# Old sums copied into PSUM by ScalarE, and four plain chunks instead of eight, in a fused attention and mixer block

## Chip, cores and metric

The kernel runs on one NeuronCore of one Trainium2 chip. The metric is device time in microseconds (us) for one execution. TensorE (PE) multiplies matrices into PSUM; VectorE (DVE), ScalarE (ACT) and GpSimd (POOL) do the rest; SyncE (SP) issues most DMAs. PEld is the weight load of TensorE.

## What is computed

```python
x = A_x                                   # 1 x 2048 x 576, float32
xn = _layernorm(x)
return x + _A_ref(xn, A_wqkv, A_wo) + _B_ref(xn, B_w1, B_w2, B_w3, B_w4)
```

`_A_ref` is attention with 32 heads of 18 channels, in which every token looks at 8 tokens: itself and those 2, 4, ... 14 places before it. `_B_ref` is a mixer: `h = gelu(layernorm(xn) @ w1)`, four channel groups shifted by 1, -1, 2, -2 tokens, `x1 = xn + hs @ w2`, and then `x1 + gelu(layernorm(x1) @ w3) @ w4` with a hidden width of 4608.

## The kernel before, in words

**Precision.** Every float32 operand is kept as a high part (rounded to `float32r`) and a low part (the remainder), and a product is three products: high by high, high by low, low by high. A contraction over 576 channels is therefore 14 matmuls (`PAIRS`), one over 128 hidden channels 3. Making the two parts is a cast on ScalarE and a subtraction on VectorE; the functions named `split_...` and `low_part` (L815) do that.

**Stages.** First QKV: for each tile of 128 tokens, `q_half` (L319) makes one half of the 1728 columns at a time, 864 of them, as two accumulations of 432 columns in two PSUM banks (`mm_tok`, L211); ScalarE copies them out (L323) and they are stored to `qkvd` in DRAM. Tiles 4 to 15 go this way, the first four through `q_cg`. Then the first mixer (L466 to L500), then `w2` (the loop at L621), whose result is the running sum `Y`, 16 tiles of 128 tokens. Then the hidden layer of the second mixer, which is by far the longest stage, and at last the product with `wo` (L1335 on).

**The running sum.** For the tiles in `YD` (1, 2, 3, 5, 7, 9, 10, 11, 13, 15) the sum lives in DRAM (`yd`), and the space of these tiles in `Y` serves as scratch (`temp`; the raw W4 is loaded to the places of tiles 1 and 3). The other six tiles (0, 4, 6, 8, 12, 14) are summed in `Y` in SBUF. `down` (L830) makes the contribution of 256 hidden channels to one tile: 12 matmuls of 288 columns into a two-bank PSUM tile. For a YD tile ScalarE copies it out (L846), and GpSimd issues a DMA that adds it to `yd` (L847). For another tile VectorE adds PSUM to `Y` (L851).

**The hidden layer** has 36 blocks of 128 hidden channels; two make a chunk, 18 chunks. The first `NPL` (8) are *plain*: a unit is one chunk by 512 tokens. In a unit, two `up`s (L819) of 14 matmuls of 512 columns each give the hidden values, ScalarE applies GELU twice from PSUM (L805, L806), VectorE makes the low part (L817), and then four downs follow for the unit before (`prev`). PSUM tiles of the downs come from a pool of three (`psb`).

The other chunks (`NWP`, 10) use a fast scheme with seven products instead of eight: two chunks' worth of output, 256 hidden channels by 1024 tokens, is one *step* `q` of the loop at L1140, 2 x `NWP` steps in all, the first `NWP` for the first half of the tokens (`sb` 0), the others for the second. `product` (L1069) is 7 matmuls of 512 columns. Their weights are sums and differences made on chip: `load_pair` (L915) loads a pair of blocks into the staging tile `w3st` (one buffer), `split_a` (L944) makes the operands A (`w3a`, two buffers), `combine` (L926) forms the differences in place on VectorE, `split_s` (L950) makes the operands S (`w3s`). In `split_ws` (L934) step 0 is a cast (L936) and step 1 another cast and a GpSimd DMA that accumulates (L939). The token operands (`B11`, `B21`, `T1` ... `T4`, `B22`) are loaded by `get_op` (L885) and split by `split_op` (L895), seven for each half; the sums `T` over normalised tokens are made in DRAM by `sums` (L868).

**The order of a step** is written out by hand as a string (`ORDER`, L1135, and `ORDERS` for steps 0, `NWP` - 1 and `NWP`): P1 to P7 are the seven products and D0 to D7 the eight downs of the step before. What else is done after which item stands in `plan` (`at(...)`, L1174 on). P1, P6, P7 and P4 add up in one PSUM bank (`ca`), and in between `keep` (L1080) copies the bank to SBUF: P1 gives Z1, P6 gives Z2, P7 gives Z3. P2 and P1 together give hidden values: P2 has its own bank, VectorE adds it to Z1 (`z_add`, L1083), and `gelu_z` (L809) takes them from SBUF. The same is done for Z2 and Z3 with P3's bank. The downs have two PSUM tiles (`qpd`). Every engine works through its instructions in the order in which they are written, with waits on semaphores.

**Attention** (L677) runs on VectorE in the background from unit 2 on, eight groups of four heads. It is a generator; each `yield` names the cost of what it has issued in us, and `bg` (L772) lets it go on while its budget lasts: 9.4 us per plain unit (`RATE`), and 1.6 us less what is already `spent` per item of a step. `av` sums the weighted values of a group in `po[:, 0]` and stores it to `od`. The softmax's exp is on ScalarE (L755). In step `NQ` - 6, after P4, whatever is left is done at once, and `od` is loaded, transposed and split for the last product.

Of the kernel before, what the change touches and what calls it, by code (L numbers as in the profile page):

```python
# [19 lines left out]
HD = 18  # L20
# [16 lines left out]
NPL = 8  # L37
# [20 lines left out]
def fused_block(ctx, tc, x, wqkv, wo, w1, w2, w3, w4, out):  # L58
# [487 lines left out]
    def split_w3(f):  # L546
        if f // 2 % 2 == 0:
            W3[f] = wp.tile([128, 15, 128], F32R, name="w3a", bufs=2)[:, 0:10, :]
        elif f % 2 == 0:
            t = wspool.tile([128, 20, 128], F32R, name="w3s")  # L550
            W3[f], W3[f + 1] = t[:, 0:10, :], t[:, 10:20, :]
        split_w(W3[f][:, 0:5, :], W3[f][:, 5:10, :], raws[f])
# [124 lines left out]
    def attention(ap):  # L677
# [8 lines left out]
        o = po[:, 0, :].rearrange("p (x d) -> p x d", d=HD)  # L686
# [12 lines left out]
        def av(g):  # L699
            if g == NG - 1:  # L700
                exp_now()
            L, v = Ls[g], vs[g]
            Lf = L.rearrange("p j h w -> p (j h) w")
# [6 lines left out]
            for w in range(W):  # L710
# [5 lines left out]
                if w:  # L716
# [3 lines left out]
                         po[:, 0, :].rearrange("p (j c) -> p j c", c=GC))  # L720
# [107 lines left out]
    nps = [0]  # L828

    def down(t, parts, pd):  # L830
        col = slice(t % 4 * 128, (t % 4 + 1) * 128)
        if pd is None:
            nps[0] += 1
            ps = qpd.tile([128, 2, 512], F32, name=f"ps{nps[0] % 2}")
        else:
            ps = pd.tile([128, 2, 512], F32, name="ps", tag="b")
# [3 lines left out]
        for n, (h, w, p) in enumerate(seq):  # L840
            for k in range(2):
                pe.matmul(ps[:, k, :HF], h[:, col], w[:, p, k * HF:(k + 1) * HF],  # L842
                          start=n == 0, stop=n == len(seq) - 1)
# [4 lines left out]
        else:  # L848
            spent[0] += 0.75
            yv = Y[:, t, :].rearrange("p (h c) -> p h c", h=2)  # L850
            dve.tensor_tensor(yv, ps[:, :, :HF], yv, op=ALU.add)  # L851
# [11 lines left out]
    def add_x(t):  # L863
        if t not in YD:
            dve.tensor_tensor(Y[:, t, :], Y[:, t, :], xagain[t], op=ALU.add)
# [97 lines left out]
    RATE = [9.4, 0.0]  # L963
# [5 lines left out]

    for u, (c, b) in enumerate(units):  # L970
        if u == 2:
# [9 lines left out]
        for i in range(C):  # L981
            bg(r, False)
# [28 lines left out]
        for j, (t, parts) in enumerate(prev):  # L1011
            bg(r, j % 2 == 1)
            down(t, parts, psb)
# [7 lines left out]
            for f in {(-3, 1): (lambda: split_a(0),), (-3, 3): (lambda: combine(0),),  # L1021
# [14 lines left out]
        if z == -5:  # L1036
            load_pair(0)
        if z == -3:
# [5 lines left out]
        if z == -2:  # L1044
# [5 lines left out]
            load_w4(NPL)  # L1050
        if 5 <= u < 21 and u % 2:
            sums((u - 5) // 8, (u - 5) % 8 // 2)
        if 13 <= u < 13 + NT:
            load_xa(u - 13)
        if 14 <= u < 14 + NT:
            add_x(u - 14)
# [6 lines left out]
    qpd = qpdc.__enter__()  # L1063
    Z1, Z2, Z3, Z4 = temp(13), temp(15), temp(5), temp(7)
# [22 lines left out]
    def downs(g):  # L1087
        s0 = 8 * (g // NWP)
        w1, w0 = W4[2 * (NPL + pair(g))], W4[2 * (NPL + pair(g)) + 1]
        for j in range(8):  # L1090
            if j < 4:
                yield lambda j=j: down(s0 + 4 + j, [(hid[g, "c12"], w0), (hid[g, "c22"], w1)], None)
            else:
                yield lambda j=j: down(s0 + j - 4, [(hid[g, "c11"], w0), (hid[g, "c21"], w1)], None)

    def plain_downs():
        for t, parts in prev:
            yield lambda t=t, parts=parts: down(t, parts, None)
# [31 lines left out]
    def o_turn(t):  # L1130
# [4 lines left out]
    ORDER = "P1 P2 D0 P6 D1 P5 D2 P7 D3 P4 D4 P3 D5 D6 D7"  # L1135
    ORDERS = {0: "P1 P2 D0 P6 P5 P7 D1 D2 P3 P4 D3",
              NWP - 1: "P1 P2 P6 P5 P7 D0 P4 P3 D1 D2 D3 D4 D5 D6 D7",
              NWP: "D0 D1 P1 P2 D2 P6 D3 P5 P7 D4 P4 P3 D5 D6 D7"}
    spent[0] = 0.0
    for q in range(NQ):  # L1140
# [36 lines left out]
        if q == 0:  # L1177
            at("P2", split_op, 0, "B22")
            at("P5", split_op, 0, "T4")
            at("P7", split_a, n, (0, 1))  # L1180
            at("D1", gelu22)
            at("D1", split_a, n, (2,))
            at("D2", low22)
            at("P3", combine, n)
# [4 lines left out]
            at("D3", split_w4, p)  # L1189
            at("D3", load_pair, q + 2)  # L1190
        elif q == NWP - 1:
# [5 lines left out]
            at("D0", split_op, 1, "B11")  # L1197
# [23 lines left out]
        elif z < -1:  # L1221
# [6 lines left out]
            at("P4", split_w4, p, 1)  # L1228
            at("D4", low22)
# [162 lines left out]
```

## Time and profile before

| | us |
|---|---|
| median of 3 runs | 1294.18 (1293.34 to 1298.37) |
| the profiled execution's own time | 1294.18 |
| its span, first to last instruction | 1292.4 |
| TensorE busy | 1267.1 |
| VectorE busy | 944.7 |
| ScalarE busy | 598.7 |
| GpSimd busy | 246.3 |

The mean granted TensorE clock is 0.994 of full speed; in the page's 40 slices it is full except for one in the middle of the last third. The difference between the execution's time and the span is what lies around the first and last instruction. QKV ends at about 195 us of the span, the plain stage runs from about 313 to 719 and the steps from there to about 1215, with the last downs to 1230.

How to read the rows that follow: a row of the timeline is start, duration, engine, line, operation, output and inputs, shape and count, and in brackets the idle time before it and what ended it. Neighbouring instructions of one kind are merged. A row of the groups ends with total busy time, mean ns of one, and the idle time before. A row of the waits is total, times and longest. A row of the windows is the stretch, its length, and the busy time of PE, PEld, DVE, ACT and POOL, then granted clock, DMA share and GB/s. A row of the DMA issues ends with the KB of one and the median us from issue to landing. Matmuls overlap, so their pace is read from start to start and not from their duration.

### The profile page before, as it was taken

The numbers are of one execution on the slowest core, as the hardware profiler recorded it, in microseconds if no ns is written. First come the engines' busy times: TensorE is split into PE (matmuls) and PEld (weight loads), VectorE is DVE, ScalarE is ACT, GpSimd is POOL, SyncE is SP. The second block draws the span as 40 slices with busy tenths as digits, with TensorE's granted clock in tenths as the row PEclk, the third lists the DMA queues.
The fourth block names the chain that finished last, engine by engine and source line by source line (L and its number), as shares of the span: only waits on it lengthen the run. The fifth ranks groups of instructions, "written<-read, shape, count | busy, mean of one in ns | idle before, by whom it ended". The sixth has DMA issues, their size and how long they took to land.

```text
span 1292.4 us, 19686 instructions
## 1 busy us (share of the span) xinstructions
PE 1267.1 (98%) x7538; PEld 1163.1 (90%) x7538; DVE 944.7 (73%) x1261; ACT 598.7 (46%) x952; POOL 246.3 (19%) x358
## 2 busy tenths in 40 slices
PE   8999999999999999999999999999979999999999
PEld 8999998899898998999999799989968999988998
DVE  6456534778469999999999789989978554566542
ACT  3322126526634434343345746546547555555530
POOL 2011100021221212231212212222212222222100
PEclk9999999999999999999999999999989999999999
DMA  7646874246886878989788767686595757799972
GB/s 210 156 113 139 171 173 143 73 131 174 220 245 148 180 165 202 229 154 222 136 200 204 168 136 163 112 191 154 106 261 87 155 102 154 178 218 222 254 250 83
DMA packets 201374, 219.16 MB, mean 170 GB/s; under 512 B 79152, under 2 KB 137744, under 8 KB 201152
## 3 DMA queue, kind: packets, MB, share of 16 engines
q1 hardware_dynamic: 168912, 151.57, 40.9%
q0 software_dynamic: 32368, 66.34, 32.2%
q8 instruction: 59, 0.97, 0.3%
q14 instruction: 35, 0.29, 0.1%
HBM read 119.73 MB, written 107.28 MB: 176 GB/s over the span
## 4 chain that ended last, share of the span: by engine, by line
PE 74%; DMA 8%; issue 7%; DVE 6%; ACT 2%; SPq 2%; POOL 1%; DVEq 0%; POOLq 0%; ACTq 0%
PE ps L842 26%; PE ps L214 16%; PE cc L1075 12%; PE p L823 12%; PE ps L466 4%; PE ps L313 3%; DMA yd<-Y 2%; DMA w3st<-in_B_w_dram 1%; DMA Y<-in_B_w_dram 1%; DMA w3a<-w3st 1%; DVE w L569 1%; DMA od<-po 1%; PE ps L481 1%; DVE w3st L931 1%; DMA w3s<-w3st 1%
## 5 line engine op out<-in xcount | busy, mean ns | idle before, releaser
L842 PEld LDWEIGHTS ps<-w,c 128*128 128x128 f32 x3456 | 474.9, 188 | 28.1 <-DVE Y L851 7.7
L842 PE MATMUL ps<-w,c 128*128 128x288 f32 x3456 | 486.4, 295 | 11.9 <-DVE Y L851 5.6
L847 POOL DMA_DIRECT2D yd<-Y x154 | 137.3, 897 | 453.9 <-ACT Y L846 378.6
L846 ACT COPY Y<-ps 128x576 f32<-128x576 f32 x154 | 98.1, 637 | 141.8 <-PE ps L842 90.4
L817 DVE TENSOR_TENSOR c<-Y,c 128x512 fp32r<-128x512 f32 x144 | 98.5, 685 | 60.0 <-ACT Y L806 49.9
L214 PE MATMUL ps<-WQ,xt 128*128 128x432 f32 x672 | 134.8, 360 | 0.0
L214 PEld LDWEIGHTS ps<-WQ,xt 128*128 128x128 f32 x672 | 125.6, 188 | 5.7
L851 DVE TENSOR_TENSOR Y<-ps,Y 128x576 f32<-128x576 f32 x108 | 81.1, 751 | 48.8 <-PE ps L842 48.5
L1075 PE MATMUL cc<-xt,w3s 128*128 128x512 f32 x420 | 108.8, 400 | 0.0
L737 DVE TENSOR_TENSOR po<-q,k 128x2304 f32<-128x2304 f32 (+1 forms) x40 | 82.9, 2073 | 16.1 <-issue 10.9
L805 ACT ACTIVATE c<-p 128x512 fp32r<-128x512 f32 x64 | 38.3, 599 | 119.3 <-PE p L823 119.3
L1075 PEld LDWEIGHTS cc<-xt,w3s 128*128 128x128 f32 x420 | 77.4, 192 | 14.1 <-DVE Y L1085 0.2
L740 DVE TENSOR_REDUCE L<-po 128x128 f32<-128x2304 f32 (+1 forms) x40 | 82.7, 2068 | 0.4
L1081 ACT COPY Y<-cc 128x512 f32<-128x512 f32 x60 | 35.1, 585 | 100.7 <-PE cc L1075 94.9
L121 POOL TENSOR_TENSOR rs<-rs,mhalf 128x1 f32<-128x1 f32 x48 | 31.6, 659 | 258.1 <-DVE rs L120 147.8
L717 DVE TENSOR_TENSOR po<-po 128x1152 f32<-128x1152 f32 x56 | 75.8, 1353 | 0.9
L713 DVE TENSOR_TENSOR po<-v,L 128x1152 f32<-128x1152 f32 x56 | 75.6, 1352 | 0.7
L323 ACT COPY stg<-ps 128x864 f32<-128x864 f32 x24 | 21.2, 882 | 102.8 <-PE ps L214 55.8
L1075 PE MATMUL cc<-x1n,w3a 128*128 128x512 f32 (+1 forms) x280 | 67.9, 393 | 0.0
L1075 PEld LDWEIGHTS cc<-x1n,w3a 128*128 128x128 f32 (+1 forms) x280 | 51.6, 188 | 10.3
L214 PE MATMUL ps<-W,h 128*128 128x288 f32 x384 | 53.5, 295 | 0.0
L823 PE MATMUL p<-xt,w3s 128*128 128x512 f32 x224 | 52.4, 390 | 0.0
(189 smaller groups left out, 1904.3 us busy)
## 6 DMA issues: line engine op xcount, KB each, us to landing
yd<-Y POOLq DMA_DIRECT2D x156, 288.0 KB, 5.3
Y<-in_B_w_dram SPq DMA_DIRECT2D x27, 576.0 KB, 6.9
w3st<-in_B_w_dram SPq DMA_DIRECT2D x52, 256.0 KB, 6.4
qkvd<-stg SPq DMA_DIRECT2D x24, 432.0 KB, 3.5
yd<-ev POOLq DMA_DIRECT2D x26, 288.0 KB, 6.2
xd<-st SPq DMA_DIRECT2D x16, 320.0 KB, 6.0
xd<-big SPq DMA_DIRECT2D x16, 320.0 KB, 7.9
w3st<-in_B_w_dram SPq DMA_DIRECT2D x76, 64.0 KB, 6.6
```

Of the source, the lines that this page charges most:

```text
L214: pe.matmul(ps[:, h, :n], xs(a), ws(b, h), start=i == 0, stop=i == len(PAIRS) - 1)
L713: dve.tensor_tensor(dst, vv, Lf[:, :, w:w + 1].to_broadcast([128, TPP * GH, HD]), op=ALU.mult)
L717: dve.tensor_tensor(o, o, dst, op=ALU.add)
L737: dve.tensor_tensor(dst, qf[:, None, :].to_broadcast([128, n, TPP * GC]), win, op=ALU.mult)
L740: dve.tensor_reduce(Lw[:, w:w + n, :], dst.rearrange("p w (x d) -> p w x d", d=HD), axis=AX.X, op=ALU.add)
L817: dve.tensor_tensor(h[:, 1, :], g, h[:, 0, :].bitcast(F32), op=ALU.subtract)
L823: pe.matmul(ps, W3[f][:, w, :], x1n[b][:, a, :], start=n == 0, stop=n == len(PAIRS) - 1)
L842: pe.matmul(ps[:, k, :HF], h[:, col], w[:, p, k * HF:(k + 1) * HF], start=n == 0, stop=n == len(seq) - 1)
L846: act.copy(e.rearrange("p (h c) -> p h c", h=2), ps[:, :, :HF])
L847: pool.dma_start(yd[t], e, accum_op=ALU.add)
L851: dve.tensor_tensor(yv, ps[:, :, :HF], yv, op=ALU.add)
L1075: pe.matmul(ps, WX[w][:k, v, SLOT[w], :], area[sb][xk][:k, a, :], start=onto is None and i == 0, stop=last and i == len(HALVES) - 1, skip_ ...
```

## The change

- `NPL` goes from 8 to 4, so 16 plain units instead of 32 and 28 steps instead of 20 (`NWP` 14).
- A tile outside `YD` gets its old sum into PSUM before its matmuls: `ahead` lets ScalarE copy `Y` into the next PSUM tile, three downs ahead in the plain stage and two in the steps; the matmuls add to it (no `start`), and ScalarE copies the sum back to `Y`. The add on VectorE (L851) is gone.
- From step 1 on, P2 adds to a copy of P1's bank (`cb`), which ScalarE makes; GELU takes it from PSUM, and P1's `keep`, one `z_add` and the GELU from Z1 are gone. D0 stands between P1 and P2.
- `q_half` makes its 864 columns as 512 + 352, and ScalarE copies them out as one run.
- W4 of the first pair is loaded after unit `NU` - 4 and split in unit `NU` - 3 (before: loaded after unit `NU` - 2, split in D3 of step 0).
- In step 0 the split of the next A operand is done at P1 and P6 (before P7 and D1), `combine` at D2 (before P3). In the regular steps the second half of W4's split goes from P4 to D4. In step `NWP` - 1 the order and the place of B11's split change.
- The last attention group sums its output into the group's `q` tile instead of `po`.
- `sums`, the reload of x and its adds are placed anew to fit 16 units; the budget of attention becomes 12.4 us per unit less what is `spent`, and W3's split and the adds of x count as spent.

```diff
-NPL = 8
+NPL = 4
@@ q_half
-        mm_tok(ps, lhs(t), lambda b, i: WQ[:, b, (2 * h + i) * CG:(2 * h + i + 1) * CG], CG)
+        xs, c = lhs(t), 2 * h * CG
+        for i, (a, b) in enumerate(PAIRS):
+            for k, (n0, n1) in enumerate(((0, 512), (512, 2 * CG))):
+                pe.matmul(ps[:, k, :n1 - n0], xs(a), WQ[:, b, c + n0:c + n1],
+                          start=i == 0, stop=i == len(PAIRS) - 1)
-        act.copy(stg.rearrange("p (i c) -> p i c", i=2), ps[:, :, :CG])
+        act.copy(stg, ps.rearrange("p i c -> p (i c)")[:, :2 * CG])
@@ av
+            o, out = (o_, po[:, 0, :]) if g < NG - 1 else (
+                qs[g].rearrange("p j (h d) -> p (j h) d", d=HD), qs[g].rearrange("p j d -> p (j d)"))
@@ before down
+    bank = {"order": [], "next": 0, "open": [], "make": None}
+    def halves(t):
+        return Y[:, t, :].rearrange("p (h c) -> p h c", h=2)
+    def ahead():
+        n = bank["next"]
+        if n < len(bank["order"]):
+            t = bank["order"][n]
+            ps = bank["make"](n)
+            if t not in YD:
+                act.copy(ps[:, :, :HF], halves(t))
+            bank["open"].append((t, ps))
+            bank["next"] = n + 1
+    def begin_downs(order, bufs, make):
+        assert not bank["open"] and bank["next"] == len(bank["order"])
+        bank.update(order=order, next=0, make=make)
+        for _ in range(bufs):
+            ahead()
@@ down
+        due, ps = bank["open"].pop(0)
-                          start=n == 0, stop=n == len(seq) - 1)
+                          start=n == 0 and t in YD, stop=n == len(seq) - 1,
+                          skip_group_check=True)
...
-            spent[0] += 0.75
-            yv = Y[:, t, :].rearrange("p (h c) -> p h c", h=2)
-            dve.tensor_tensor(yv, ps[:, :, :HF], yv, op=ALU.add)
+            act.copy(halves(t), ps[:, :, :HF])
+        ahead()
@@ plain stage
-    RATE = [9.4, 0.0]
+    RATE = [12.4, 0.0]
+    XADD = {5: 0, 6: 4, 7: 8, 8: 12, 10: 6, 12: 14}
+        if u == 1:
+            begin_downs([4 * units[v][1] + j for v in range(NU - 1) for j in range(4)], 3,
+                        lambda n: psb.tile([128, 2, 512], F32, name="ps", tag="b"))
-            bg(r, False)
+            bg(r - spent[0], False)
+            spent[0] = 0.0
-            for f in {(-3, 1): (lambda: split_a(0),), (-3, 3): (lambda: combine(0),),
+            for f in {(-3, 1): (lambda: split_a(0),), (-3, 2): (lambda: split_w4(NPL),),
+                      (-3, 3): (lambda: combine(0),),
+        if z == -4:
+            load_w4(NPL)
-            load_w4(NPL)
-        if 5 <= u < 21 and u % 2:
-            sums((u - 5) // 8, (u - 5) % 8 // 2)
+        if 4 <= u < 12 and u % 2 == 0:
+            sums(0, (u - 4) // 2)
@@ steps
+    begin_downs([4 * units[NU - 1][1] + j for j in range(4)]
+                + [8 * (g // NWP) + (j + 4) % 8 for g in range(2 * NWP) for j in range(8)], 2,
+                lambda n: qpd.tile([128, 2, 512], F32, name=f"ps{n % 2}"))
-    ORDER = "P1 P2 D0 P6 D1 P5 D2 P7 D3 P4 D4 P3 D5 D6 D7"
+    ORDER = "P1 D0 P2 P6 D1 P5 D2 P7 D3 P4 D4 P3 D5 D6 D7"
     ORDERS = {0: "P1 P2 D0 P6 P5 P7 D1 D2 P3 P4 D3",
-              NWP - 1: "P1 P2 P6 P5 P7 D0 P4 P3 D1 D2 D3 D4 D5 D6 D7",
-              NWP: "D0 D1 P1 P2 D2 P6 D3 P5 P7 D4 P4 P3 D5 D6 D7"}
+              NWP - 1: "P1 D0 P2 P6 P5 P7 D1 P4 P3 D2 D3 D4 D5 D6 D7",
+              NWP: "D0 D1 P1 D2 P2 P6 D3 P5 P7 D4 P4 P3 D5 D6 D7"}
@@ step 0
+            at("P1", split_a, n, (0, 1))
             at("P2", split_op, 0, "B22")
+            at("P6", split_a, n, (2,))
             at("P5", split_op, 0, "T4")
-            at("P7", split_a, n, (0, 1))
-            at("D1", split_a, n, (2,))
             at("D2", low22)
-            at("P3", combine, n)
+            at("D2", combine, n)
-            at("D3", split_w4, p)
@@ step NWP - 1, then the regular steps
-            at("D0", split_op, 1, "B11")
+            at("D1", split_op, 1, "B11")
-            at("P4", split_w4, p, 1)
+            at("D4", split_w4, p, 1)
+        if 0 < q < 5:
+            at("D2", sums, 1, q - 1)
@@ items of a step
             if it == "P1":
                 ca = product("A11", "B11", q % 2 * 3)
-                keep(Z1, ca)
+                if q:
+                    cb = qpc.tile([128, 512], F32, name="cc1")
+                    act.copy(cb, ca)
+                else:
+                    keep(Z1, ca)
             elif it == "P2":
-                cb = product("A12", "B21", 1, last=True)
-                z_add(Z1, cb, Z1)
+                if q:
+                    product("A12", "B21", onto=cb, last=True)
+                else:
+                    cb = product("A12", "B21", 1, last=True)
+                    z_add(Z1, cb, Z1)
             elif it == "P6":
                 product("S2", "T2", onto=ca)
+                if q:
+                    h11 = hid[q, "c11"] = gelu_ps("c11", cb, Z1)
                 keep(Z2, ca)
             elif it == "P5":
                 cc = product("S1", "T1", 2)
-                h11 = hid[q, "c11"] = gelu_z("c11", Z1)
+                if q:
+                    low_part(h11, Z1)
+                else:
+                    h11 = hid[q, "c11"] = gelu_z("c11", Z1)
```

More of the change, by code (lines that the diff above doesn't have):

```diff
@@ L826, in up, with down @@
         low_part(h, g)
-    nps = [0]
-    def down(t, parts, pd):
-        col = slice(t % 4 * 128, (t % 4 + 1) * 128)
[L832 to L836, printed above, removed]
+    bank = {"order": [], "next": 0, "open": [], "make": None}
[15 more added lines that the diff above has]
+            ahead()
+    def down(t, parts):
+        col = slice(t % 4 * 128, (t % 4 + 1) * 128)
+        due, ps = bank["open"].pop(0)
+        assert due == t
         seq = []
@@ L1011, in fused_block @@
         for j, (t, parts) in enumerate(prev):
[L1012 to L1013 removed]
+            bg(r - spent[0], j % 2 == 1)
+            spent[0] = 0.0
+            down(t, parts)
             if (u, j) == (2, 0):
```

25 lines of the change are left out of this document (15 added, 10 removed).

## The prediction

> **What bounds the kernel now.** I read the page's busy times and its chain of waits first, then the timeline of TensorE alone, stage by stage.
>
> ```profile
> PE 1267.1 (98%) x7538; PEld 1163.1 (90%) x7538; DVE 944.7 (73%) x1261; ACT 598.7 (46%) x952; POOL 246.3 (19%) x358
> PE 74%; DMA 8%; issue 7%; DVE 6%; ACT 2%; SPq 2%; POOL 1%; DVEq 0%; POOLq 0%; ACTq 0%
> ```
>
> TensorE is busy for 98% of the span and carries 74% of the chain. So the time is the sum of its matmuls plus its waits; whatever another engine saves counts only where TensorE waits for it. The next rows (start, duration, instruction, count) give its pace.
>
> ```profile
> 680.00 6.55 PE L823 MATMUL p<-x1n,w3s 128*128 128x512 f32 x28
> 692.72 6.55 PE L823 MATMUL p<-xt,w3s 128*128 128x512 f32 x28
> ...
> 790.51 3.39 PE L1075 MATMUL cc<-x1n,w3a 128*128 128x512 f32 x14
> 793.74 1.75 PE L842 MATMUL ps<-w,c 128*128 128x288 f32 x12
> 795.33 1.78 PE L1075 MATMUL cc<-xt,w3s 128*128 128x512 f32 x7
> ...
> 814.60 1.78 PE L1075 MATMUL cc<-x1n,w3a 128*128 128x512 f32 x7
> ```
>
> A plain unit takes 12.72 us (680.00 to 692.72). A seven-product step, which does the work of two units, takes 24.09 (790.51 to 814.60). In it a product takes 3.23 / 2 = 1.62 and a down 1.59. These are the stalls that the change touches:
>
> ```profile
> PE ps L842 <- DVE Y L851: 5.6, 8, 1.2
> ```
>
> (TensorE's waits in total: time, times, longest) and, from the timeline,
>
> ```profile
> 736.29 3.39 PE L1075 MATMUL cc<-x1n,w3a 128*128 128x512 f32 x14
> 741.68 0.53 PE L842 MATMUL ps<-w,c 128*128 128x288 f32 x2 [2.00 <-ACT w L566]
> 743.07 2.77 PE L842 MATMUL ps<-w,c 128*128 128x288 f32 x10 [0.86 <-DVE w L569]
> 766.45 1.79 PE L1075 MATMUL cc<-x1n,w3a 128*128 128x512 f32 x7
> 948.92 1.36 DVE L713 TENSOR_TENSOR po<-k,L 128x1152 f32<-128x1152 f32 x1 [7.60 <-DMA od<-po]
> 952.73 3.35 PE L1075 MATMUL cc<-xt,w3a 128*128 128x512 f32 x7 [6.32 <-ACT Y L1081]
> 958.16 8.19 PE L842 MATMUL ps<-w,c 128*128 128x288 f32 x60
> ```
>
> Step 1 takes 30.16 (736.29 to 766.45), 6.1 more than a step: 2.86 of waits for the split of W4, and 3.2 in which the matmuls ran at half pace. Step 9 waits 6.32 because VectorE stood 7.60 for a store of `po`; its next two products then take 5.43 (952.73 to 958.16) instead of 3.24, so 8.5 in all.
>
> **The change, part by part.** All sums start at the profiled execution, 1294.18 us (span 1292.4); it is also the median of the three runs.
>
> **Four plain chunks fewer.** Sixteen units become eight steps: 8 x (2 x 12.72 - 24.09) = -10.8.
>
> **The stalls of before.** W4 of the first pair is now loaded after unit 12 and split in unit 13, instead of loaded after unit 30 and split in the last down of step 0.
>
> ```profile
> Y<-in_B_w_dram SPq DMA_DIRECT2D x27, 576.0 KB, 6.9
> ```
>
> Landing takes 6.9, and the ups of unit 13 (6.4) with two downs lie between, so it lands in time, and its two casts have 30 us of cover: -6.1. The last attention group sums into `q` instead of `po`, so no store stands before its first product: -8.5. The adds of L851 leave VectorE: -5.6. The old sums over `xn` and the reloads of x are packed into units 4 to 13; the sums end at unit 10, their first reader is loaded after unit 13, 38 us later. On GpSimd's queue they stand between the accumulates into `yd`, and GpSimd is 19% busy: nothing. Attention: by the planner's own costs 357 us are needed, some 92 fit into the plain stage, 14 into each later step, and the last one ends in step 21; the flush is in step 22: nothing, and some 10 us late if the costs were 5% short.
>
> **QKV in 512 + 352.** One pair of matmuls keeps its 864 columns.
>
> ```profile
> 63.69 11.26 PE L214 MATMUL ps<-WQ,xt 128*128 128x432 f32 x56
> 74.79 0.60 PE L136 MATMUL ps<-ident,Y 128*128 128x128 f32 x4
> 206.54 12.86 PE L466 MATMUL ps<-xt,W 128*128 128x512 f32 x56
> 219.24 1.07 PE L481 MATMUL ps<-xt,W1R 128*128 128x512 f32 x4
> ```
>
> Start to start, 432 columns take 11.10 / 56 = 198.2 ns, 512 take 226.8, and 288 take 1.59 / 12 = 132.5. 352 is not in the trace: it lies between 132.5 and 198.2. The line from 288 (the nearer row) to 512 gives 159; 432 lies 5 ns above that line. A pair is then 386 instead of 396: 336 pairs (12 tiles, 2 halves, 14) x -10.6 ns = -3.6, with ends of -12.5 and +9.6. The Trainium skill (TensorE: Matmul & The Clock Gate, Back-to-back issue gap) has a gap of N / 2.4 + 2.5 ns, so 182.5 for 432 and 215.8 + 149.2 for the new pair: it gives no gain at all, and the three measured pitches disagree with it.
>
> **ScalarE's new work.** For each tile outside YD, ScalarE copies the old sum in (new) and the new one out, instead of one add on VectorE.
>
> ```profile
> L846 ACT COPY Y<-ps 128x576 f32<-128x576 f32 x154 | 98.1, 637 | 141.8 <-PE ps L842 90.4 <-issue 37.3 <-DMA yd<-Y 11.4
> L199 ACT CAST Wo<-wr 128x576 fp32r<-128x576 f32 x5 | 3.4, 675 | 0.0
> 1019.56:1043.62 24.06, 24.06 (x147) 21.94 (x146) 12.16 (x17) 13.21 (x21) 5.93 (x8) 1.00 0.62 124
> ```
>
> A copy from SBUF into PSUM isn't in the trace; the nearest rows are 637 (out of PSUM) and 675 (SBUF to SBUF), and I take 0.64. A step has three such tiles: 3 x 1.28 = 3.8 on top of 13.2 busy of 24.06 (the fourth group of numbers in the windows row is ScalarE). In a regular step I cost it at nothing: the bank is filled two downs ahead, the copies lie beside products, and D0 comes after P1, which covers the copy of the first product (0.6, before P2) too. The cover is thin where downs follow one another: a copy out and in takes 1.5 of a down's 1.59, so anything else in ScalarE's queue is then paid in full. Three places have that.
>
> **Step 0.** The split of the next A operand moves from P7 to P1, where ScalarE waits for a load.
>
> ```profile
> 717.28 0.78 POOL L939 DMA_DIRECT2D w3s<-w3st  x1 [9.67 <-ACT w3s L938]
> 718.62 3.40 PE L1075 MATMUL cc<-x1n,w3a 128*128 128x512 f32 x14
> 720.00 0.97 SPq L920 DMA_DIRECT2D w3st<-in_B_w_dram  x2
> 721.02 2.56 SPq L923 DMA_DIRECT2D w3st<-in_B_w_dram  x4
> w3st<-in_B_w_dram SPq DMA_DIRECT2D x52, 256.0 KB, 6.4
> w3st<-in_B_w_dram SPq DMA_DIRECT2D x76, 64.0 KB, 6.6
> ```
>
> The staging tile has one buffer, free only after the accumulate at 717.28, and the change doesn't touch that. The last small load is issued at about 721.02 + 0.75 x 2.56 = 722.9 and lands at 729.5. Until then ScalarE stands in P1's split, and behind it queue the split of B22 (2.3), D0's copy out and a copy in (0.5 each, pipelined) and the copy of P6's sum (0.6), which ends at 734.1. P7 adds to that same bank and would start at 718.62 + 4 x 1.62 + 1.59 = 726.7. TensorE waits 7.4 and runs on at half pace, 2.2 as after the 6.32: +9.6, at most 12 with 3.2 and a later load, at least nothing, if the load is early.
>
> **Steps 13 and 14**, where the second half's operands are split. These rows of step 9 show the same place:
>
> ```profile
> 959.95 0.64 ACT L846 COPY Y<-ps 128x576 f32<-128x576 f32 x1 [5.00 <-PE ps L842]
> 960.48 1.06 ACT L902 ACTIVATE x1n<-x1n 128x1024 fp32r<-128x1024 f32 x1
> ...
> 962.76 1.14 ACT L566 CAST w<-Y 128x1152 fp32r<-128x1152 f32 x1
> 963.80 0.62 ACT L846 COPY Y<-ps 128x576 f32<-128x576 f32 x1
> 964.33 0.63 ACT L811 ACTIVATE c<-Y 128x512 fp32r<-128x512 f32 x1
> ...
> 965.53 1.04 ACT L902 ACTIVATE xt<-xt 128x1024 fp32r<-128x1024 f32 x1
> ...
> 972.97 1.85 PE L842 MATMUL ps<-w,c 128*128 128x288 f32 x12 [0.94 <-ACT Y L846]
> ```
>
> Start to start a copy takes 0.53, an operand's split 2.28, W4's 1.04, a GELU pair 1.20. From D2's end in step 13 to P2 of step 14, ScalarE has 8 copies out, 3 in, 5 splits, W4, 2 pairs and the product's copy: 4.2 + 1.6 + 11.4 + 1.0 + 2.4 + 0.6 = 21.2, TensorE 7 x 1.59 + 1.62 + 1.59 = 14.3. The excess is 7 with 0.2 of latency; 1.3 follows at P7, whose bank waits for a copy behind the split of B22. The same counting gives 2.1 for step 9, where 1.2 was measured, so I take off 0.8: 7.5. Of before's waits there, 0.9 was ScalarE's: +6.6, bounds 1 and 11.
>
> **The end.** After the last step, eleven downs run in a row beside the splits of Wo and the attention output.
>
> ```profile
> 1221.31 1.85 PE L842 MATMUL ps<-w,c 128*128 128x288 f32 x12 [0.46 <-ACT Y L846]
> ```
>
> Counted alike: the first of the last eight downs waits for D6's copy out and in behind a GELU pair (0.5), the third for the first one's behind the last pair (0.7), the fourth for the second one's behind 2.3 of casts (1.1). These 2.3 take the place of this 0.46: +1.8.
>
> **Sum**: -10.8 - 6.1 - 8.5 - 5.6 - 3.6 + 9.6 + 6.6 + 1.8 = -16.6, so 1278.
>
> **The rivals.** (a) P1's split in step 0 stops nothing: the load lands before ScalarE gets to it, and the 9.6 isn't paid: 1268. For it: half of these loads land sooner than the median. Against: issue at 720.00 comes only 1.4 after P1 starts. (b) The waits in step 14 halve the clock as those of step 1 did (3.2), and the queue drains later by as much again: 1284. For it: 2.00 + 0.86, with matmuls between, did it; against: my waits are spread, the longest 2.1. The Trainium skill (TensorE: Matmul & The Clock Gate, Why this matters for your kernels) puts the limit at an idle gap of about 3 us; by it these waits are harmless, but step 1 had no single gap of that size, and there the trace disagrees. (c) Matmuls cost by columns with one fixed part, so 512 + 352 is 2 x 432 and the 3.6 is not gained: 1281. The pitches at 288, 432 and 512 speak against it; this is what the page's formula amounts to. (d) Slower: in every step, one GELU pair stands ahead of a copy out in the run D5 D6 D7, with the copies in behind it, and TensorE pays its 1.2: 27 x 1.2 = 32, so 1310. It decides from 16.6 / 27 = 0.6 us a step. For it: ScalarE has 17.0 of 24.1, and some 20 in a step with exp. Against: in the run D5 D6 D7 only D6's bank is refilled, for a D0 that comes one product later than D7.
>
> **How the numbers follow.** Forecast 0.48, (a) 0.15, (b) 0.15, (c) 0.12, (d) 0.10. The likeliest is 1278. The range, 1264 to 1289, takes in (a) with a cheaper 352, and (b) with a dearer one; (d) is outside. About 0.5%, 6.5 us, is what a measurement can tell here: faster means under 1287.7. Forecast, (a), (c) and most of (b) are: 0.83; same 0.09; slower 0.08.
>
> **What would show it.** In the profile after: 24.1 between the P1 of regular steps; no wait for L566 or `od<-po`; a PE wait of 5 to 8 in step 0 ended by ScalarE's copy of P6's sum, with a ScalarE wait for `w3st` loads before it; several waits of 1 to 2 around D5 of step 13 to P7 of step 14; QKV pairs at 386 ns. I am wrong if regular steps exceed 24.7, if step 0 runs through, or if VectorE, with more attention in each unit, delays the low parts that downs need.

## The result and the profile after

The changed kernel takes 1312.49 us, the median of six runs (1309.02 to 1313.82); the kernel before took 1293.78 beside it. The ratio is 1.0135 [1.0113, 1.0157]: **slower by 1.35%**, where 1278 was forecast. The profiled execution of after is 1313.82 (span 1312.0), so 35.8 us have to be found. The page's busy times and its chain by engine come first.

```profile
PE 1263.2 (96%) x7482; PEld 1148.2 (88%) x7482; DVE 905.5 (69%) x1194; ACT 766.1 (58%) x1220; POOL 259.1 (20%) x374
PE 63%; DMA 14%; issue 8%; ACT 6%; DVE 5%; SPq 2%; POOL 2%; POOLq 0%; ACTq 0%; DVEq 0%
```

TensorE still sets the end, but transfers have gone from 8% to 14% of the chain and ScalarE from 2% to 6%. The waits of TensorE (total, times, longest) say on whom:

```profile
PE ps L865 <- ACT Y L870: 21.4, 9, 8.5
PE cc L1112 <- ACT Y L1118: 9.4, 3, 8.2
PE cc L1112 <- ACT cc L1304: 2.3, 2, 1.5
```

The waits of before for L851, for L566 and for the store of `po` are gone. In their place stand a few long ones for ScalarE. First what went as forecast, in the timeline of after, on TensorE:

```profile
63.63 11.28 PE L324 MATMUL ps<-WQ,xt 128*128 128x512 f32 x56
74.75 0.60 PE L136 MATMUL ps<-ident,Y 128*128 128x128 f32 x4
...
692.00 1.78 PE L1112 MATMUL cc<-x1n,w3a 128*128 128x512 f32 x7
716.05 1.79 PE L1112 MATMUL cc<-x1n,w3a 128*128 128x512 f32 x7
...
883.31 3.58 PE L865 MATMUL ps<-w,c 128*128 128x288 f32 x24 [2.01 <-ACT Y L870]
899.82 1.89 PE L1112 MATMUL cc<-x1n,w3a 128*128 128x512 f32 x7 [1.46 <-ACT cc L1304]
```

A regular step takes 24.05 (692.00 to 716.05), although ScalarE now copies sums in and out beside it: that costs nothing, as forecast. Steps 13 and 14 have waits of up to 2.01 and no half pace behind them: the granted clock is 1.00 from 860 to 910. The waits there come to 6.8, where 7.5 was counted. From start to start, the two steps lose 9.6 (57.67 from 860.90 to 918.57, in place of 48.1). In the kernel before, steps 9 and 10 lose 2.2 beside the 8.5 for `po` (58.91 from 936.59 to 995.50), so this is +7.4, where +6.6 was counted. The QKV isn't as forecast: 56 matmuls take 11.12 (63.63 to 74.75), a pair 397 ns, against 396 before.

Now the lost time. Step 0, with ScalarE's row among TensorE's:

```profile
534.88 3.40 PE L1112 MATMUL cc<-x1n,w3a 128*128 128x512 f32 x14
545.95 0.83 ACT L960 CAST w3a<-w3st 128x768 fp32r<-128x768 f32 x1 [8.66 <-DMA w3st<-in_B_w_dram]
551.31 3.30 PE L1112 MATMUL cc<-x1n,w3s 128*128 128x512 f32 x7 [8.21 <-ACT Y L1118]
562.44 1.79 PE L1112 MATMUL cc<-x1n,w3a 128*128 128x512 f32 x7
```

Step 0 takes 27.56 in place of 17.7: +9.9, and 9.6 was forecast, by this very chain (load, split, copy of P6's sum, P7). The delays of two of the last eight plain units were not forecast. Unit 8:

```profile
413.82 6.55 PE L830 MATMUL p<-xt,w3a 128*128 128x512 f32 x28
417.04 0.90 POOL L901 DMA_DIRECT2D td0T<-xn  x1 [5.33 <-issue]
417.62 1.15 POOL L880 DMA_DIRECT2D yd<-in_A_x_dram  x1
423.71 2.67 POOL L871 DMA_DIRECT2D yd<-Y  x3 [4.93 <-issue]
430.10 0.64 ACT L870 COPY Y<-ps 128x576 f32<-128x576 f32 x1 [7.47 <-DMA yd<-Y]
430.79 3.25 PE L865 MATMUL ps<-w,c 128*128 128x288 f32 x12 [5.67 <-ACT Y L870]
433.84 7.06 PE L830 MATMUL p<-xt,w3a 128*128 128x512 f32 x28
```

GpSimd's queue stands for 5.33 and 4.93 around a packed sum (L901) and a reload of x (L880). So the three accumulates behind them are issued late, their staging buffers come free late, ScalarE's copy out (L870) waits 7.47, and the down behind it 5.67. The next down takes 3.04 (430.79 to 433.84), half pace. The unit takes 20.02 in place of 12.73. Unit 14, the last but one:

```profile
492.94 2.55 DVE L744 TENSOR_TENSOR po<-q,k 128x2304 f32<-128x2304 f32 x1
495.52 0.34 SPq L697 DMA_DIRECT2D q<-qkvd  x1
495.91 0.79 SPq L697 DMA_DIRECT2D k<-qkvd  x1
497.27 0.38 SPq L915 DMA_DIRECT2D x1n<-xn  x1
497.99 6.55 PE L830 MATMUL p<-xt,w3s 128*128 128x512 f32 x28
510.47 1.06 ACT L926 ACTIVATE x1n<-x1n 128x1024 fp32r<-128x1024 f32 x1 [7.99 <-DMA x1n<-xn]
517.80 3.25 PE L865 MATMUL ps<-w,c 128*128 128x288 f32 x12 [8.51 <-ACT Y L870]
520.84 7.86 PE L830 MATMUL p<-xt,w3s 128*128 128x512 f32 x28
```

Operand B11 is loaded from 497.27 on, right behind attention's q and k, and is there at 510.47: 13.2. ScalarE comes to its split 7.99 too early and holds up the copies behind it; the unit takes 22.85. The issue itself is late: SyncE can send q only when VectorE has used the old q for the last time (492.94 + 2.55 = 495.49; q goes out at 495.52), and B11's loads stand behind it in SyncE's order. And step 1:

```profile
570.86 0.53 SPq L895 DMA_DIRECT2D td1T<-xn  x1
584.04 1.15 DVE L955 TENSOR_TENSOR w3st<-w3st 128x384 f32<-128x384 f32 x2 [5.86 <-DMA w3a<-w3st]
586.45 1.05 ACT L960 CAST w3s<-w3st 128x1024 fp32r<-128x1024 f32 x1 [4.14 <-PE ps L865]
588.70 3.25 PE L865 MATMUL ps<-w,c 128*128 128x288 f32 x12 [2.27 <-ACT Y L870]
591.74 1.89 PE L1112 MATMUL cc<-x1n,w3a 128*128 128x512 f32 x7
```

Behind the four copies of 576 KB for the second half's sums (L895 is the first), the accumulate into `w3a` lands late: VectorE's combine waits 5.86 for it, ScalarE's split follows, and D7 waits 2.27. Step 1 takes 29.30 (562.44 to 591.74), 5.2 over a regular one; the four steps up to 692.00 take 3.9 over theirs.

| where the 35.8 us are | us |
|---|---|
| unit 8 (+7.3) and unit 9 (+0.5) | 7.8 |
| unit 14 (+10.1) and unit 15 (+1.3) | 11.4 |
| steps 1 to 5: 5.2 + 3.9 | 9.1 |
| units 0 to 2 (a wait of 2.65 at 332.76 in place of 1.55, then half pace) | 3.0 |
| QKV, where 3.6 was counted as a gain | 3.6 |
| step 0, 9.9 instead of 9.6 | 0.3 |
| steps 13 and 14, 7.4 instead of 6.6 | 0.8 |
| sum | 36.0 |

### The profile page after: what moved, and what is told of

It is laid out like the page before. It is cut to its first block, busy times and chain, and to the rows that moved or that the text cites. A ratio compares the mean times of both kernels' runs of the same rounds, so it can differ in the third digit from the quotient of the medians.

```text
span 1312.0 us, 20032 instructions
## 1 busy us (share of the span) xinstructions
PE 1263.2 (96%) x7482; PEld 1148.2 (88%) x7482; DVE 905.5 (69%) x1194; ACT 766.1 (58%) x1220; POOL 259.1 (20%) x374
## 4 chain that ended last, share of the span: by engine, by line
PE 63%; DMA 14%; issue 8%; ACT 6%; DVE 5%; SPq 2%; POOL 2%; POOLq 0%; ACTq 0%; DVEq 0%
PE ps L865 20%; PE cc L1112 12%; PE ps L324 10%; PE p L830 6%; PE ps L214 6%; PE ps L470 4%; DMA w3st<-in_B_w_dram 3%; PE ps L313 3%; DMA w3a<-w3st 3%; DMA x1n<-xn 2%; POOL yd L871 1%; DMA Y<-in_B_w_dram 1%; DMA Y<-od 1%; DMA yd<-Y 1%; DVE w3st L955 1%
## 5 line engine op out<-in xcount | busy, mean ns | idle before, releaser
L1112 PE MATMUL cc<-xt,w3s 128*128 128x512 f32 (+1 forms) x588 | 149.3, 393 | 0.0
L870 ACT COPY Y<-ps 128x576 f32<-128x576 f32 x154 | 97.7, 636 | 74.7 <-PE ps L865 56.9
L324 PE MATMUL ps<-WQ,xt 128*128 128x512 f32 (+1 forms) x672 | 134.9, 360 | 0.0
L1112 PEld LDWEIGHTS cc<-xt,w3s 128*128 128x128 f32 (+1 forms) x588 | 107.6, 188 | 21.1 <-DVE Y L1122 0.4
L1112 PE MATMUL cc<-x1n,w3a 128*128 128x512 f32 x392 | 100.1, 395 | 2.3 <-ACT cc L1304 2.3
L873 ACT COPY Y<-ps 128x576 f32<-128x576 f32 x108 | 68.9, 638 | 39.8 <-PE ps L865 38.4
L1112 PEld LDWEIGHTS cc<-x1n,w3a 128*128 128x128 f32 x392 | 70.7, 188 | 15.1 <-ACT cc L1304 2.7
L955 DVE TENSOR_TENSOR w3st<-w3st 128x384 f32<-128x384 f32 x108 | 60.2, 557 | 27.2 <-issue 16.1
L846 ACT COPY ps<-Y 128x576 f32<-128x576 f32 x108 | 69.6, 645 | 2.7
L1122 DVE TENSOR_TENSOR Y<-cc,Y 128x512 f32<-128x512 f32 x57 | 39.1, 685 | 32.7 <-ACT Y L1118 27.9
L1112 PE MATMUL cc<-x1n,w3s 128*128 128x512 f32 (+1 forms) x196 | 51.6, 404 | 8.7 <-ACT Y L1118 8.7
```

Of the source, the lines that this page charges most:

```text
L324: pe.matmul(ps[:, k, :n1 - n0], xs(a), WQ[:, b, c + n0:c + n1], start=i == 0, stop=i == len(PAIRS) - 1)
L870: act.copy(e.rearrange("p (h c) -> p h c", h=2), ps[:, :, :HF])
L955: dve.tensor_tensor(st[:, :, o, :], st[:, :, o, :], st[:, :, i, :], op=op)
L1112: pe.matmul(ps, WX[w][:k, v, SLOT[w], :], area[sb][xk][:k, a, :], start=onto is None and i == 0, stop=last and i == len(HALVES) - 1, skip_ ...
```

## Theories and experiments

**Theory**: ScalarE's new work is harmless; the time goes where a transfer lands late and ScalarE, which works in order, stands before it. The packed sums and reloads, the earlier split in step 0, and the place of attention's loads make these transfers late. **Rival**: ScalarE, at 58%, is the cost itself, and a wait that is taken away comes back elsewhere.

**Undoing one part of the change.** Step 0's splits where the kernel before has them:

```diff
-            at("P1", split_a, n, (0, 1))
-            at("P6", split_a, n, (2,))
-            at("D2", combine, n)
+            at("P7", split_a, n, (0, 1))
+            at("D1", split_a, n, (2,))
+            at("P3", combine, n)
```

> The changed kernel, with step 0's split of the next A operand and its combine back at P7, D1 and P3. Theory (the rest of the loss is late landings in front of an in-order ScalarE): TensorE's wait of 8.2 us in step 0 goes, with the half clock behind it, so 9 to 10 us less than the changed kernel's 1312.5, about 1303. Rival (ScalarE simply has too much to copy): the copies of the old sums are still there, the wait moves to the next product or to step 1, and less than 3 us come back.

1302.92 us, 1.0077 [1.0058, 1.0097]: 9.6 less than after, as both the prediction's term and the trace had it.

The reloads of x into `yd` out of the units:

```diff
-        if 4 <= u < 4 + len(YD):
-            load_xa(YD[u - 4])
...
+        if 15 <= q < 25:
+            at("D4", load_xa, YD[q - 15])
```

> The changed kernel, with the ten reloads of x into yd taken out of units 4 to 13 and put into steps 15 to 24, one each. Theory: in unit 8 the reload and the sums stand in GpSimd's queue before the accumulates into yd, whose staging tiles ScalarE waits for; without the reloads the wait of 5.7 us and its half clock go, 7 to 8 us less, about 1305. Rival (ScalarE's own work): no change, within 2 us of 1312.5.

```profile
412.67 6.55 PE L830 MATMUL p<-xt,w3a 128*128 128x512 f32 x28
425.39 6.55 PE L830 MATMUL p<-xt,w3a 128*128 128x512 f32 x28
```

In the timeline of this run, unit 8 takes 12.72: its wait is gone, so the reloads did cause it. GpSimd's queue still stands 8.16 and 4.67 at the packed sum, but without the reload the accumulates go out in time. The total, 1310.33 us (1.0129 [1.0108, 1.015]), moved by only 2.2, less than expected, and its interval overlaps that of after; the profiled run, the fastest of the four, has a span of 1305.8, 6.2 less than after's. How much of the unit's 7.8 comes back in other runs stays open.

Attention's pace in the plain stage, so that its loads fall elsewhere:

```diff
-    RATE = [12.4, 0.0]
+    RATE = [11.4, 0.0]
```

> The changed kernel with attention's budget 11.4 instead of 12.4 us per plain unit, so that the loads of group 3's q and k fall behind the plain stage instead of ahead of the operand loads after unit 13. Theory: the operand loads land some 5 us sooner, the wait of 8.5 us in unit 14 goes with its half clock: 9 to 11 us less, about 1302. Rival: ScalarE's backlog in unit 14 comes from its own casts, and less than 3 us are gained.

```profile
488.08 0.93 SPq L915 DMA_DIRECT2D x1n<-xn  x1
498.61 6.55 PE L830 MATMUL p<-xt,w3s 128*128 128x512 f32 x28
511.39 3.81 PE L830 MATMUL p<-xt,w3s 128*128 128x512 f32 x16
...
896.46 1.06 ACT L926 ACTIVATE xt<-xt 128x1024 fp32r<-128x1024 f32 x1 [6.25 <-DMA xt<-td1T]
901.29 2.05 PE L865 MATMUL ps<-w,c 128*128 128x288 f32 x7 [7.56 <-ACT ps L846]
```

1320.15 us, 1.0194 [1.0166, 1.0222]: a miss, and a useful one. Unit 14 takes 12.78 (498.61 to 511.39), so the place of attention's loads was what made it late. B11's first load is issued at 488.08, 9.2 sooner than in after, and lands after 10.5 in place of 13.2: most of the delay was the late issue, and 2.7 of it the slower landing. But attention's loads now stand ahead of the operand loads of step 13, and 7.56 is paid there, with half pace behind it: the collision moved. Smaller waits for ScalarE that after doesn't have, the longest 2.54 (610.29), make up the rest.

The kernel before, with the QKV in 512 + 352 alone:

> The kernel before, with the 864 columns of a QKV half as 512 + 352 alone. By the prediction's line through 288 and 512 columns it gains 3.6 us (ratio 0.997); by the changed kernel's trace, where 28 pairs take 11.09 us as 28 pairs of 432 did, it gains nothing (1.000).

1295.09 us, 1.0012 [0.9999, 1.0026]: no gain, which is rival (c).

**All four moves together.** Step 0 as in the first run, reloads as in the second, attention at 11.0 (by the planner's costs, the pace at which no load of it is issued just ahead of an operand's), and the second half's sums one DMA per step:

```diff
-        if 0 < q < 5:
-            at("D2", sums, 1, q - 1)
+        if 0 < q < 9:
+            at("D2", sums1, q - 1)
```

> The kernel after with four moves of loads and operands, the computation unchanged: step 0's operands are split where the kernel before did it (P7, D1, combine at P3); GpSimd's ten reloads of x go to steps 15 to 24; attention's rate is 11.0, so that no load of it is issued just ahead of operand B11's loads or of steps 13 and 14's; the second half's packed sums are spread, one DMA per step over steps 1 to 8. Theory (the 35.8 us are transfers that land late and hold up ScalarE's in-order queue, not ScalarE's own work): step 0 gives back 9.9, unit 8 gives back 7.8, unit 14 gives back 11.4, steps 1 to 4 give back 5 or more of 9.2, so 1312.5 - 34 = 1279, and with some new meeting of two loads up to 1285: faster than the kernel before by 0.7 to 1.2%. Rival (ScalarE at 58% busy is itself the cost, the waits only move): 1300 or more.

1282.09 us, 0.9907 [0.9871, 0.9943]: 30.4 less than after with the same arithmetic, faster than before. ScalarE does the same work (765.7 busy in place of 766.1), so the rival falls for these 30.4. The moves don't add up one by one: alone, step 0's gave back 9.6, the reloads 2.2 and the spread sums 3.8 (below), and the pace at 11.4 cost 7.7. The windows of this run and of after, over units 13 and 14 (fourth group of numbers ScalarE, then clock, DMA share and GB/s behind GpSimd's):

```profile
487.00:521.00 34.00, 34.00 (x202) 30.81 (x201) 22.89 (x26) 30.34 (x48) 8.53 (x10) 1.00 0.97 229
```

```profile
487.00:521.00 34.00, 25.49 (x147) 23.30 (x146) 23.26 (x22) 18.75 (x30) 6.31 (x8) 0.89 0.94 240
```

The DMA engines are as full in the good run, first row, as in after, second row (0.97 and 0.94). So their load doesn't decide here; when the one load that ScalarE needs is issued, and what stands ahead of it, does.

The spread sums alone, in the kernel after:

> The kernel after, and the second half's packed sums (four copies of 576 KB and four accumulates, issued in steps 1 to 4) issued one per step over steps 1 to 8. Theory (the four copies of one step fill the queues ahead of the load that step 1's split waits for): step 1 comes down from 29.3 to about 25 us, steps 3 to 5 lose most of their 4 us, 1312.5 - 6 = 1306 (1304 to 1309). Rival (the accumulates themselves are slow, wherever they stand): no change, 1311 to 1314.

```profile
559.39 1.79 PE L1123 MATMUL cc<-x1n,w3a 128*128 128x512 f32 x7
584.80 1.79 PE L1123 MATMUL cc<-x1n,w3a 128*128 128x512 f32 x7
```

Step 1 takes 25.41, as expected. The total is 1308.71, 1.0107 [1.0062, 1.0152]: 3.8 less than after, and the two intervals overlap.

**Another queue.** The loads of the first three operands issued by GpSimd instead of SyncE:

```diff
             for k in ("B11", "B21", "T3"):
-                get_op(0, k)
+                get_op(0, k, pool)
```

> The kernel after, with the twelve DMAs of the first half's first three operands (ahead of unit 14) issued on GpSimd's queue in place of SyncE's, behind which attention's q and k of group 3 stand in the kernel after. Theory (a queue's transfers land in order, so a load waits for the ones issued ahead of it on its queue): unit 14's wait of 8.51 us goes, with the half clock behind it, and the time is 1312.5 - 11 = 1301. Rival (the 16 DMA engines are shared by all queues and are busy with small packets): the loads land as late, 1310 to 1314.

1316.64 us, 1.0174 [1.0152, 1.0196]; unit 14 waits 10.62. This decides less than hoped: B11's loads took 7.4 to 7.7 in place of 13.1 to 13.5, but GpSimd, behind in its own queue, issued them from 503.32 on, 6 later, so they landed at the same time. Whether a queue's order or shared engines made the landing slow stays open; that attention's loads made unit 14 late is shown by the run with its pace changed.

**The prediction's terms by themselves, in the kernel before.** W4 of the first pair early, and the last attention group summed into `q`:

```diff
+            o, out = (o_, po[:, 0, :]) if g < NG - 1 else (
+                qs[g].rearrange("p j (h d) -> p (j h) d", d=HD), qs[g].rearrange("p j d -> p (j d)"))
...
+            for f in {(-3, 1): (lambda: split_a(0),), (-3, 2): (lambda: split_w4(NPL),), (-3, 3): (lambda: combine(0),),
...
+        if z == -4:
             load_w4(NPL)
...
-            at("D3", split_w4, p)
```

> The kernel before, with eight plain chunks, VectorE's adds and its own QKV, and two of the change's small parts alone: the first pair's W4 is loaded in the fourth unit from the end and split in the third, and the last attention group sums into q in place of a tile in PSUM. Theory (the terms of the prediction stand: 6.1 us of the W4 wait in step 1 and 8.5 us of the wait for the last group's output in step 9): 1294.2 - 14.6 = 1279.6 (1278 to 1284), ratio 0.989. Rival (a wait taken away is followed by another one of the same length, as in the kernel after): 1288 to 1295.

```profile
743.08 1.33 PE L844 MATMUL ps<-w,c 128*128 128x288 f32 x8 [1.45 <-DVE c L819]
761.70 3.44 PE L844 MATMUL ps<-w,c 128*128 128x288 f32 x24 [1.19 <-DVE Y L853]
...
950.50 3.34 PE L844 MATMUL ps<-w,c 128*128 128x288 f32 x24
956.07 1.85 PE L844 MATMUL ps<-w,c 128*128 128x288 f32 x12 [2.23 <-ACT Y L848]
960.26 9.73 PE L844 MATMUL ps<-w,c 128*128 128x288 f32 x60 [2.34 <-DVE Y L853]
```

1293.16 us, 0.9984 [0.9967, 1.0]: of 14.6 expected, 1.4 came. In its timeline, both waits are gone, but in step 9 the operand splits are late next: 2.23 + 2.34, and 60 matmuls in 9.73 in place of 60 x 0.1325 = 7.95. ScalarE stands 6.67 there for the first operand's load (at 953.13) before it can split it, so this is a transfer again. In step 1, 1.45 for VectorE is left in place of 2.00 and 0.86, and 1.19 comes 18 us later. Here the rival's "it comes back elsewhere" holds.

ScalarE's copies of old sums alone, in the kernel before (the functions `ahead`, `begin_downs` and `down` of the change):

> The kernel before, with its eight plain chunks, and one part of the change alone: ScalarE puts a token tile's old sum into PSUM ahead and copies the result out, in place of VectorE's add from PSUM. Theory (a copy ahead costs nothing in a regular step, and in the two steps in which ScalarE splits the next operand it costs 5 to 6 us; VectorE's waits give back 5.6, the end takes 1.8): 1292 to 1298, within 0.3% of the kernel before. Rival (ScalarE's copies are the change's cost): 1305 or more, since 35.8 us are missing in the kernel after.

```profile
PE ps L858 <- ACT Y L863: 7.0, 6, 1.6
PE cc L1100 <- ACT Y L1106: 5.1, 6, 1.1
PE ps L858 <- ACT w L566: 3.3, 1, 3.3
```

1302.69 us, 1.0053 [1.003, 1.0076]: 8.1 dearer, between theory and rival. TensorE's longest waits in this run are for ScalarE's copies out (7.0 in six), its copies of products (5.1 in six) and one split of W4 (3.3, in place of 2.00 before). The price of the copies isn't isolated by it: attention, which no longer gives way to the adds, also runs ahead (the store of `po` of 939.81 is issued at 902.59), and the wait of 6.32 behind that store comes to 1.91. One add of x moves by a unit, too.

The same part undone in the good version, so that VectorE adds:

```diff
-            act.copy(halves(t), ps[:, :, :HF])
+            spent[0] += 0.75
+            dve.tensor_tensor(halves(t), ps[:, :, :HF], halves(t), op=ALU.add)
```

> The kernel of the run e_spread, 1282.1 us, with the change's main part undone: VectorE adds a token tile's old sum from PSUM, as in the kernel before; no copy into PSUM ahead, no copy out. Four plain chunks, the QKV, the second product onto a copy, and the moved loads stay. Theory (the run h_before_copies: the copies cost 8.4 us where everything else is as before): 1274 (1271 to 1278), ratio to the kernel before 0.984. Rival (the prediction's term: VectorE's adds are late, and the copies give 5.6 back once the transfers are out of their way): 1284 to 1290.

```profile
1136.13 4.21 PE L863 MATMUL ps<-w,c 128*128 128x288 f32 x16 [59.54 <-DVE Y L872]
```

1345.41 us, 1.0394 [1.0375, 1.0413]: neither theory nor rival. One wait of 59.54 holds nearly all of it: the planner charges the adds to VectorE's time, attention isn't done when step 22 needs it, and the rest of it runs there in one piece. Up to that place the run is only about 3 behind e_spread. Whether the adds would fit with another pace of attention was not tried.

With VectorE's adds in steps 13 and 14 alone:

```diff
+            copied = t not in YD and not (len(bank["order"]) > 100 and 12 <= (n - 4) // 8 < 14)
```

> The kernel of the run e_spread, with VectorE's adds only for the six token tiles in SBUF of steps 13 and 14, where ScalarE splits the second half's operands. Theory (ScalarE's copies are late only there: waits of 2.02, 0.97 and 1.45 at 846 to 863 us): 1282 - 3 = 1279. Rival (operand splits alone fill ScalarE's queue there): 1281 to 1283.

**1277.63 us, 0.9865 [0.9847, 0.9883]**: the best version, faster than both kernels. Its four runs (1275.48 to 1278.07) all lie below the five of e_spread (1280.45 to 1284.14), so here ScalarE's copies did cost some 4.5, as the prediction's term for these steps has it in kind.

The second product in a bank of its own again:

```diff
-                    product("A12", "B21", onto=cb, last=True)
+                cb = product("A12", "B21", 1, last=True)
+                z_add(Z1, cb, Z1)
```

> The kernel of the run e_spread, with one small part of the change undone: the product of A12 and B21 starts a bank of its own and VectorE adds it to the first one, in place of matmuls that add to ScalarE's copy of the first. Theory (that part was costed at nothing in regular steps): 1282, within 3 us. Rival (the copy, which matmuls wait for, costs something in every step): 1276 or less; rival (VectorE's added 0.69 us in each step is late): 1287 or more.

1312.69 us, 1.0136 [1.0116, 1.0157]: 30.6 dearer than e_spread, for 27 additions of 0.69 = 18.6 us on VectorE. The suspect is VectorE's room. In the windows of e_spread, it (third group) is busy for 228.59 of 240; two rows of this run follow:

```profile
600.00:840.00 240.00, 239.78 (x1439) 217.88 (x1438) 228.59 (x229) 178.27 (x277) 62.20 (x73) 1.00 0.86 184
```

```profile
1115.49 0.83 ACT L971 CAST w3a<-w3st 128x768 fp32r<-128x768 f32 x1 [6.55 <-DMA w3st<-in_B_w_dram]
1119.89 3.36 PE L1121 MATMUL cc<-xt,w3a 128*128 128x512 f32 x7 [5.21 <-ACT Y L1127]
```

The longest wait of TensorE in this run, 5.21, is not for VectorE itself: ScalarE stands 6.55 for weights whose loads go out late (1109.42). They stand in SyncE's order behind the loads of attention's output (issued from 1102.02, in e_spread from 1073.79), and those wait for attention's last group, whose last addition starts at 1093.6 in place of 1054.6. The waits of 3.57 (1173.72) and 3.65 (726.92) have a late load behind them as well.

Two more runs tested it: the best version with eight plain chunks, and that one without the accumulation.

```diff
-NPL = 4
+NPL = 8
```

> The kernel of the run j_spread_relief, 1277.6 us, with eight plain chunks in place of four (as in the kernel before, with its own places for the sums, the reloads and attention); ScalarE's copies with VectorE's adds in the two steps that split operands, the second product onto a copy, W4 early, the last group's sum in q and the QKV in 512 + 352 stay. Theory (the prediction's term for the four chunks, 10.8 us, is right, and what j gains over the kernel before beyond it comes from the other parts): 1288 (1286 to 1291). Rival (the other parts are worth little, since each wait that goes is followed by another, as in g_before_two_waits): 1292 to 1298, and the four chunks are worth 15 or more.

> The kernel m_eight_chunks with the second product in a bank of its own and VectorE adding it, as in l_spread_no_onto. Theory (what cost 30 us in l_spread_no_onto is VectorE's room: with four plain chunks attention fills VectorE until 1094 us; with eight, it ends near 950 and 0.69 us more in each step is free): the same as m_eight_chunks, within 3 us. Rival (the addition by VectorE makes matmuls wait wherever it stands): 12 us or more above m_eight_chunks, for 20 steps in place of 28.

1294.82 us, 0.9994 [0.9978, 1.0011], and 1298.04 us, 1.003 [1.0014, 1.0045]. With eight chunks the addition on VectorE costs 3.2, with four 30.6: its price depends on VectorE's room, and what is paid is in good part late loads again. The last group's sums on VectorE, in e_spread and in m_eight_chunks (the span of the group stands before its shapes):

```profile
L724 DVE TENSOR_TENSOR q<-q,po x7: 1349/1354/1358, 1028.8 to 1054.6; 128x1152 f32<-128x1152 f32 x7
```

```profile
L723 DVE TENSOR_TENSOR q<-q,po x7: 1350/1357/1358, 903.9 to 930.7; 128x1152 f32<-128x1152 f32 x7
```

With eight chunks attention ends 124 us earlier. And the version with four chunks is 17.2 faster (1294.82 - 1277.63). 10.8 of it are the matmuls, as predicted, whose paces are unchanged. The other 6.4 go with waits of the version with eight: 3.62 in step 1 (747.44) and 2.46 in unit 18 (554.78), each with half pace behind it, where j_spread_relief waits 1.18 in step 1 (537.00) and has no such wait in its units. Whether another placement at eight chunks would lose them was not tried.

## Why the prediction was wrong

**The step that failed** is the one that costed transfers at nothing: "On GpSimd's queue they stand between the accumulates into `yd`, and GpSimd is 19% busy: nothing", and, alike, "Attention: ... nothing". The second half's sums, which the change puts into steps 1 to 4, are no term of the sum at all: the prediction lets the sums end at unit 10, which holds for the first half alone. The share of busy time of an engine says nothing of a queue that stands between its issues (5.33 and 4.93 in unit 8), and the planner's sum of attention's costs nothing of when its loads go out and what waits behind them (B11's, issued 9.2 late in unit 14). Units 8 and 14 and steps 1 to 5 cost 28.3 together; the run e_spread, which moves only transfers, attention's pace and step 0's splits, gave back 30.4, of which 9.6 are step 0's.

**The other terms**, in their order. Four chunks, -10.8: right as far as the matmuls go; the 17.2 of the runs have waits in them as well. W4 and the store of `po`, -14.6: both waits went, but by themselves they are worth 1.4, since I did not ask what was late next in step 9, though the rows of its splits were at hand. L851, -5.6: the waits went, but in the kernel before the copies made the time 8.1 longer; what they buy is VectorE's room, which the prediction did not price at all and which the four chunks need at the paces of attention that were tried. QKV, -3.6: nothing, as rival (c) had it, though its reason, one fixed part per matmul, doesn't fit the three pitches; a line through the pitches of 288 and 512 did not hold for 352. The formula of the Trainium skill (TensorE: Matmul & The Clock Gate, Back-to-back issue gap), which the page gives for isolated matmuls, has no gain either, and here the trace agrees, though the 365 ns for a pair, an estimate from it, stay below the 397 measured. Step 0, +9.6: right, by its mechanism and its size (9.9; 9.6 in the run). Steps 13 and 14: right in kind and nearly in size (+7.4 of +6.6), without the half clock of rival (b); taking off 0.8 was wrong, since the 1.2 held only the waits of step 9 and not the slower matmuls beside them. Rival (d), 1310, came near the time for a wrong reason: regular steps take 24.05.

That the best version stands at the 1278 of the forecast is luck, errors that cancel: without step 0's 9.6 and some 3 of steps 13 and 14, my working would give 1265 for it. The missing 12 are near what the W4 and `po` terms lacked (13.2), but QKV's 3.6 and the waits at eight chunks belong to the balance too, and no run adds it up.

Not settled: how a queue's order and shared engines divide the 13.2 of B11's load, why the four moves give more together than one by one, and the 3.0 lost in units 0 to 2, which no run was made for.

## What to carry to other kernels

A step moved onto an engine that works in order has to be priced by what that engine will stand before: for each load that it waits for, look up what is issued ahead of it and what that in turn waits for, not the median landing. When a wait is counted as gained, count at once what the same engines have behind it: here 14.6 of waits were worth 1.4. And work taken off a second engine may show no gain in waits and still be what makes room for the real gain; test it in the version that needs the room.

## What the hardware showed unexpectedly

- Pairs of 512 + 352 and of 2 x 432 columns take the same: 397 and 396 ns, though 512 alone takes 226.8 and 288 takes 132.5.
- A single wait of 2.27 (588.70) was followed by half pace (12 matmuls in 3.04, in place of 1.59, at a granted clock of 0.50); one of 2.01 (883.31) was not (granted clock 1.00). The length alone doesn't decide: one of 1.91 in h_before_copies (912.14) was followed by a clock of 0.52. In the kernel before, 2.00 and 0.86, with two matmuls between, were (0.50). The Trainium skill (TensorE: Matmul & The Clock Gate, Why this matters for your kernels) puts the limit at about 3 us; these rows lie below it.
- Operand B11's loads took 13.1 to 13.5 from issue to landing, 10.5 to 11.9 when they were issued 9.2 us sooner (c_rate), and 7.4 to 7.7 when GpSimd issued them 6 us later, at a DMA share of 0.94 in the first of these stretches and 1.00 in the last.
